# First attention of a fused attention and feed-forward kernel: q's transposes issued beside k's, and the third chunk's exponentials ahead of a norm's logarithm

## The chip, the cores and the metric

The kernel runs on one core of a Trainium2 chip. The metric is the device time of one execution in microseconds (us). Three executions before the change took 1340.37, 1340.40 and 1341.75 us; their median is 1340.4 us. The engines are named as in the profile: PE is TensorE (its weight loads are PEld), DVE is VectorE, ACT is ScalarE, POOL is GpSimd, and SP is SyncE, whose queue issues most of the DMAs.

## The reference, cut to what matters

```python
def rmsnorm(x, g):
    return x / np.sqrt(np.mean(x * x, axis=-1, keepdims=True) + 1e-06) * g
q_n, k_n = rmsnorm(q, g_q), rmsnorm(k, g_k)          # (8, 12, 448, 64)
scores = np.matmul(q_n, k_n.transpose(0, 1, 3, 2)) / np.sqrt(64)
attn = softmax(scores)                               # max, exp, sum + 1e-09, division
x = np.matmul(attn, v)                               # -> (3584, 768), heads side by side
...
h = np.maximum(x @ w_in, 0.0)                        # w_in (768, 2048)
out = (h * h) @ w_out                                # w_out (2048, 768)
```

Everything is float32. There are 8 batches of 12 heads; two heads of 64 columns fill the 128 partitions, so attention is done in 48 pairs of heads, six pairs to a batch.

## The kernel before, in words

The work is staged in four spans of two batches each. The **first attention** (`attention_alone`, L945) handles the 12 pairs of span 0 by itself on PE. Then each span's two products of the feed-forward follow, and the attention of the next span is threaded through the second product of the span before it. The products use one level of a Strassen-like scheme, whose weight blocks are prepared on DVE, ACT and POOL by the generator `prepare` (L556), a "tick" at a time; the first 48 ticks are spread over the first attention, the others over the first product.

The order of the instructions on each engine is the order in which the program issues them: nothing is rescheduled. Each engine works through its own queue in that order, and engines wait for one another by semaphores. So the place of a call in `attention_alone` sets its place in every engine's queue.

Within the first attention, the loop at L948 makes one **run** for each pair `i`; "the third run" is `i = 2`. A pair has 448 queries and keys, and the keys are cut into four chunks of 112. One run, from `i = 1` on, has four steps with a `yield` after each; after each `yield` the caller (L1502) issues the weight ticks that have come due.

- Step A: the loads of pair `i + 3` (on SP); `scores(i, 0)` and `scores(i, 1)`, each of which puts the scores of a chunk into a score bank by PE and then takes the exponentials of its two heads by ACT (L816 and L820); k's four transposes of the next pair, `transpose(i + 1, 1, 0)` (PE L791, then ACT's copy into `qkT`, L793); `values(i - 1, (2, 3))`, the second half of the previous pair's product of probabilities and v (PE L879); `add_up(i, 1)` (DVE L833, the sum of probabilities for the softmax's denominator); and `norm(i + 2)`, whose square is on ACT (L731) and whose sum and scaling are on DVE (L732, L733).
- Step B: q's four transposes of the next pair, `transpose(i + 1, 0, 0)` (PE L791), and ACT's copy with the gain (L795); `load_v(i + 1)` (SP L713); and `roots(i + 2)`: the logarithm and the exponential that make a reciprocal square root (ACT L742, L743), three small DVE instructions that refine it (L744 to L746), and the product that normalises q (POOL L747).
- Step C: `scores(i, 2)` and `scores(i, 3)`; `total_of(i - 1)` (PE L904, the denominators of the previous pair); `values(i, (0, 1))`; and `finish(i - 1)` on DVE (L922 to L924 make the factors, and L928 multiplies the value bank by them into `xT`).
- Step D: `add_up(i, 2)` for odd `i` (DVE L833), and `combine_x(i - 1)` (DVE, only from pair 6 on).

PSUM holds eight banks of 128 x 512 float32. The scores take two double banks in turn (`ps_s`, tag `s`): chunks 0 and 2 use one and chunks 1 and 3 the other. `ps_o` has one bank with the tag `o` and one with the tag `t` (for the totals). `ps_m` has the banks `m` and `n`; `bank(name, 0)` gives `m` and `bank(name, 1)` gives `n`. The values of an even pair are summed in `o`, those of an odd pair in `n` (L872). Both transposes, k's and q's, use bank `m`, one after the other. A bank is taken over by a new tile only when the last reader of the old one is done.

Of the kernel before, what the change touches and what calls it, by code (L numbers as in the profile page):

```python
# [10 lines left out]
F32 = mybir.dt.float32  # L11
U32 = mybir.dt.uint32
AF = mybir.ActivationFunctionType
# [331 lines left out]
def chunk_of(pt, s, j, n):  # L345

    return pt.rearrange("d (j p) -> d j p", j=n)[:, j] if s else pt.rearrange("d (p j) -> d j p", j=n)[:, j]
# [45 lines left out]
def attention_then_ffn_bounded(  # L393
# [35 lines left out]
    nc = tc.nc  # L429

    B, H, S, D = q.shape
    NT, DM = out.shape
    DFF = w_in.shape[1]
    P = 128
# [26 lines left out]
    ps_o = ctx.enter_context(tc.tile_pool(name="ps_o", bufs=1, space=bass.MemoryType.PSUM))  # L461
# [3 lines left out]
    def bank(name, n=None):  # L465

        turn[0] += n is None
        return ps_m.tile([P, S], F32, tag="mn"[turn[0] % 2 if n is None else n], name=name)

    qk, qkT, ident, mhalf, gains, rstd0, _ = held  # L470
# [209 lines left out]

    pts = {}
    vs, probs, pavs, tots, normed, rstds = {}, {}, {}, {}, {}, {0: rstd0}
    places, halves, rests = [], [], {}
    sums = {"out": [dram.tile([2 * S // 32, 32], F32, name=f"factors{n}") for n in range(2)]}

    def load(i):
        if i < NAT:
            load_q(nc, qk, q, i)
            load_k(nc, qk, k, i)
            return  # L690

        load_part(i, 0)
        load_part(i, 1)
# [15 lines left out]
    def load_v(i):  # L709
        b, h0 = i // NPAIR, 2 * (i % NPAIR)  # L710
        vs[i] = loads.tile([P, 2, NJ, D], F32, tag="vt", name="vt")
        if i < NAT:
            nc.sync.dma_start(vs[i][:SP].rearrange("p h j d -> p h (j d)"),  # L713
                              v[b, h0:h0 + 2].rearrange("h (p j) d -> p h (j d)", j=NJ))
        else:
            for h in range(2):
                nc.sync.dma_start(vs[i][:, h, 0:NF], v[b, h0 + h, 0:NF * P].rearrange("(j p) d -> p j d", j=NF))
            for rows in sides:
                nc.sync.dma_start(vs[i][rows, :, NF], v[b, h0:h0 + 2, NF * P:].rearrange("h p d -> p h d"))
# [66 lines left out]

    def transpose(i, s, n):

        pt = bank("pt", n)
        for j in range(NJ):  # L790
            nc.tensor.transpose(chunk_of(pt, s, j, NJ), normed[i][s][:, j * P:(j + 1) * P], ident[:SP, :SP])  # L791
        if s:
            nc.scalar.copy(qkT[:, i % 2, s], pt)  # L793
        else:
            nc.scalar.activation(qkT[:, i % 2, s], pt, AF.Copy, scale=gains[:, 0:1])  # L795

    def scores(i, c):


        if i >= NAT:  # L800
            sc = ps_s.tile([P, 2, 512], F32, tag="s", name="sc")
            n = S if c < NF else S // 2
            for h in range(2):
                rows = slice(h * D, (h + 1) * D)
                for m, part in enumerate(sides):
                    keys = slice(c * P + m * D, c * P + (m + 1) * D) if c < NF else slice(NF * P, S)
                    of = slice(0, S) if c < NF else slice(m * n, (m + 1) * n)
                    nc.tensor.matmul(sc[part, h, 0:n], qkT[rows, 0, 1, keys], qkT[rows, 0, 0, of], start=True, stop=True)  # L808
            pr = probs[i, c] = places[(NF * i + c) % len(places)] if c < NF else halves[i % 2]
            nc.scalar.activation(pr, sc[:, :, 0:n], AF.Exp)  # L810
            return
        at = i % 2
        sc = ps_s.tile([SP, 2, 512], F32, tag="s", name="sc")
        for h in range(2):
            rows = slice(h * D, (h + 1) * D)
            nc.tensor.matmul(sc[:, h, 0:S], qkT[rows, at, 1, c * SP:(c + 1) * SP], qkT[rows, at, 0, :],  # L816
                             start=True, stop=True)
        pr = probs[i, c] = places[(NJ * i + c) % len(places)][:SP]
        for h in range(2):
            nc.scalar.activation(pr[:, h], sc[:, h, 0:S], AF.Exp, scale=rstds[i][:, 1, 2 * c + h:2 * c + h + 1])  # L820
# [4 lines left out]
    def add_up(i, c):  # L825

        acc = acc_of(i)
        if i >= NAT and c == NF:
            for m, rows in enumerate(sides):
                part = acc[rows, :, m * S // 2:(m + 1) * S // 2]  # L830
                nc.vector.tensor_tensor(part, part, probs[i, c][rows], ALU.add)
            return
        nc.vector.tensor_tensor(acc, probs[i, 0] if c == 1 else acc, probs[i, c], ALU.add)  # L833
# [38 lines left out]
    def values(i, chunks=range(NJ)):  # L872
        if 0 in chunks:
            pavs[i] = ps_o.tile([P, S], F32, tag="o", name="pav") if i >= NAT or i % 2 == 0 else bank("pav", 1)
        if i >= NAT:
            return later_values(i)
        for c in chunks:
            for h in range(2):
                nc.tensor.matmul(pavs[i][h * D:(h + 1) * D, :], vs[i][:SP, h, c, :], probs[i, c][:, h, :],  # L879
                                 start=(c == 0), stop=(c == NJ - 1))  # L880

    def later_values(i):

        rests[i] = ps_o.tile([P, S], F32, tag="t", name="rest")
        for c in range(NF + 1):
            for h in range(2):
                for m, rows in enumerate(sides):
                    into = (rests[i] if m else pavs[i])[h * D:(h + 1) * D]
                    into = into if c < NF else into[:, m * S // 2:(m + 1) * S // 2]
                    nc.tensor.matmul(into, vs[i][rows, h, c, :], probs[i, c][rows, h, :],  # L890
                                     start=(c == 0), stop=(c == NF), skip_group_check=True)

    def added(i):

        return 3 if i % 2 and i + 1 < NAT else 2
# [16 lines left out]
    def finish(i):  # L912

        b, hp = divmod(i, NPAIR)
        x = factors = xT[:, b % 2, hp]
        if i < NAT:
            pav = pavs.pop(i)


            turned, factors = sums["turned"], sums["factors"]  # L920
            few = small.tile([P, S // 32], F32, tag="few", name="few", bufs=1)
            nc.vector.transpose(turned, tots.pop(i))  # L922
            nc.vector.reciprocal(few, turned.rearrange("p (g r) -> p g r", r=32)[:, :, 0])
            nc.vector.transpose(factors.rearrange("p (g r) -> p g r", r=32),  # L924
                                few.rearrange("p g -> p g ()").to_broadcast([P, S // 32, 32]))
        else:
            pav = rests.pop(i)
        nc.vector.tensor_tensor(x, pav, factors, ALU.mult)  # L928
        del vs[i]
# [15 lines left out]
    def attention_alone():  # L945


        for i in range(NAT):  # L948
            more = i + 1 < NAT
            if 0 < i < NAT - 3:  # L950
                load(i + 3)
            scores(i, 0)
            scores(i, 1)
            if i == 0:

                transpose(1, 1, 1)
                scores(0, 2)
                scores(0, 3)
                transpose(1, 0, 0)
                add_up(0, 1)  # L960
                norm(2)
                load_v(1)
                values(0, (0, 1))
                load(3)
                yield
                continue
            if more:
                transpose(i + 1, 1, 0)
            values(i - 1, (2, 3))
            add_up(i, 1)  # L970
            if i + 2 < NAT:
                norm(i + 2)
            elif not more:
                norm(NAT)
            yield
            if more:
                transpose(i + 1, 0, 0)
            if more:
                load_v(i + 1)
            if i + 2 < NAT:  # L980
                roots(i + 2)
            yield
            scores(i, 2)
            scores(i, 3)
            total_of(i - 1)
            values(i, (0, 1))
            finish(i - 1)
            yield
            if added(i) == 3:
                add_up(i, 2)  # L990
            combine_x(i - 1)
            if NAT <= i + 3 < NAT + 2:
                load(i + 3)
            yield
        values(i, (2, 3))
        total_of(i)
        finish(i)
        combine_x(i)

    def attention(first):  # L1000
# [3 lines left out]
        for i in range(first, last + 1):  # L1004
# [42 lines left out]
            if i > first:  # L1047
                finish(i - 1)
                combine_x(i - 1)
# [512 lines left out]
def kernel(  # L1562
# [49 lines left out]
    with tc.If(bits <= limit) as small_scores:  # L1612
        with tc.manual_schedule():
            attention_then_ffn_bounded(tc, *args, held)
# [32 lines left out]
```

## Time and profile before

| quantity | value |
|---|---|
| median of three executions | 1340.4 us |
| the profiled execution, its own time | 1337.88 us |
| its span, first to last instruction | 1336.1 us |
| PE busy | 1321.4 us (99%) |
| DVE, POOL, ACT busy | 855.1, 680.1, 486.2 us |
| PE in the first attention, first score to the first product's first matmul | 8.95 to 128.47 us |
| runs `i = 2` to `i = 10`, from the first score of one to that of `i = 11` | 25.89 to 115.73 us |

The span is shorter than the execution's own time by 1.8 us, which lie outside the first and the last instruction. PE's first score matmul of a run marks where the run begins. A matmul in float32 is two PE instructions, so the eight rows "x8" of a timeline line are four matmuls, that is two chunks of scores. The profile's end times for PE are modelled, so a stall of PE is read from the starts of its instructions.

### The profile page before, as it was taken

What the parts mean: (1) busy time and instruction counts of PE and PEld (TensorE: products, weight loads), DVE (VectorE), ACT (ScalarE), POOL (GpSimd) and SP (SyncE); (2) the same over time, 40 slices, a digit from 0 to 9 for tenths busy, and PEclk for the clock granted to TensorE, in tenths of its full rate; (3) what the DMA queues carried; (4) which work ended last, traced back from release to release, by engine and by line L of the source; (5) the groups of instructions that cost most, each with busy time, mean ns of one, the idle gap of its engine ahead of it and who ended that gap; (6) DMA issues with size and microseconds to landing.
All of it is one profiled execution on the core that took longest, in us unless ns stands there. A gap on an engine that the chain in (4) does not pass through costs nothing.

```text
span 1336.1 us, 17758 instructions
## 1 busy us (share of the span) xinstructions
PE 1321.4 (99%) x5930; PEld 698.9 (52%) x5930; DVE 855.1 (64%) x1334; ACT 486.2 (36%) x939; POOL 680.1 (51%) x544
## 2 busy tenths in 40 slices
PE   8999999999999999999999999999999999999997
PEld 3333455444446654444444755444444665556887
DVE  6998899489988233467887523457878723336553
ACT  7885656554540012255542011235554101111000
POOL 5677534467656222557774422448675522322452
PEclk9999999999999999999999999999999999999999
DMA  8887999656664433356655433345664444331333
GB/s 222 228 216 190 347 387 330 197 120 136 139 147 119 89 87 88 99 120 134 135 133 144 96 97 88 99 108 114 140 130 129 116 88 145 126 89 48 116 103 57
DMA packets 413817, 190.18 MB, mean 142 GB/s; under 512 B 282388, under 2 KB 408724, under 8 KB 413716
## 3 DMA queue, kind: packets, MB, share of 16 engines
q1 hardware_dynamic: 406164, 180.21, 51.6%
q0 software_dynamic: 4736, 8.40, 2.4%
q8 instruction: 49, 0.80, 0.3%
q10 hardware_dynamic: 2816, 0.34, 0.2%
q14 instruction: 52, 0.43, 0.1%
HBM read 155.72 MB, written 33.16 MB: 141 GB/s over the span
## 4 chain that ended last, share of the span: by engine, by line
PE 90%; DVE 4%; ACT 3%; DMA 1%; issue 1%; POOL 1%; SPq 0%; ACTq 0%; POOLq 0%
PE ps L1204 19%; PE pd L1104 11%; PE pa L1104 10%; PE pc L1104 10%; PE sc L808 7%; PE pav L890 6%; PE pb L1104 5%; PE ps L1387 3%; PE ps L1255 3%; PE pd L1359 2%; PE pc L1359 2%; PE pa L1359 2%; PE sc L816 1%; PE pd L1189 1%; PE pc L1189 1%; PE pa L1189 1%
## 5 line engine op out<-in xcount | busy, mean ns | idle before, releaser
L1076 POOL TENSOR_TENSOR gT<-gT 128x448 f32<-128x448 f32 x96 | 93.7, 978 | 258.5 <-ACT gT L1072 258.5
L773 POOL TENSOR_TENSOR half<-half,mhalf 128x28 f32<-128x28 f32 x36 | 184.8, 5133 | 69.9 <-DVE half L772 60.3
L1204 PE MATMUL ps<-gT,sw 128*128 128x448 f32 x432 | 169.3, 545 | 0.0
L1072 ACT ACTIVATE gT<-gT 128x448 f32<-128x448 f32 x96 | 55.3, 576 | 293.7 <-DVE gT L1120 293.6
L1104 PE MATMUL pa<-xT,sw 128*128 128x448 f32 x384 | 154.9, 539 | 0.0
L1204 PEld LDWEIGHTS ps<-gT,sw 128*128 128x128 f32 x432 | 80.1, 190 | 87.2 <-issue 84.6
L1204 PE MATMUL ps<-gC,sw 128*128 128x448 f32 x288 | 113.1, 546 | 0.0
L808 PE MATMUL sc<-qkT 64*64 64x448 f32 (+1 forms) x1152 | 110.2, 497 | 0.5 <-ACT pr L810 0.2
L1104 PEld LDWEIGHTS pa<-xT,sw 128*128 128x128 f32 x384 | 72.9, 190 | 70.6 <-issue 70.6
L588 POOL TENSOR_TENSOR gC<-gC 128x384 f32<-128x384 f32 x64 | 71.5, 1134 | 59.9 <-DVE gC L584 58.2
L1204 PEld LDWEIGHTS ps<-gC,sw 128*128 128x128 f32 x288 | 53.2, 190 | 59.5 <-issue 58.4
L858 POOL DMA_DIRECT2D xT<-factors x72 | 37.9, 531 | 89.1 <-DMA factors<-square 62.1
L1120 DVE TENSOR_TENSOR gT<-z,pd 128x448 f32<-128x448 f32 x32 | 19.9, 620 | 98.9 <-PE pd L1104 98.7
L810 ACT ACTIVATE pr<-sc 128x896 f32<-128x896 f32 x87 | 76.9, 909 | 11.8 <-PE sc L808 11.8
L775 POOL TENSOR_TENSOR qk<-qk,half 128x448 f32<-128x448 f32 x72 | 77.4, 1096 | 2.8
L1104 PE MATMUL pd<-xT,sw 128*128 128x448 f32 x192 | 77.8, 541 | 0.2
L1104 PE MATMUL pd<-xC,sw 128*128 128x448 f32 x192 | 77.5, 540 | 0.0
L1104 PE MATMUL pc<-xT,sw 128*128 128x448 f32 x192 | 77.4, 539 | 0.0
L1104 PE MATMUL pc<-xC,sw 128*128 128x448 f32 x192 | 77.4, 539 | 0.0
L1104 PE MATMUL pb<-xC,sw 128*128 128x448 f32 x192 | 77.4, 539 | 0.0
L890 PE MATMUL pav<-pr,vt 64*64 64x448 f32 x348 | 72.7, 537 | 0.0
L890 PE MATMUL rest<-pr,vt 64*64 64x448 f32 x348 | 72.7, 537 | 0.0
(282 smaller groups left out, 2447.6 us busy)
## 6 DMA issues: line engine op xcount, KB each, us to landing
sw<-w1s SPq DMA_DIRECT2D x224, 192.0 KB, 2.4
sw<-w2s SPq DMA_DIRECT2D x102, 256.0 KB, 3.4
w1s<-gC SPq DMA_DIRECT2D x8, 1344.0 KB, 7.0
w2s<-gC SPq DMA_DIRECT2D x8, 1344.0 KB, 6.1
qk<-in_q_dram SPq DMA_DIRECT2D x144, 56.0 KB, 2.5
qk<-in_k_dram SPq DMA_DIRECT2D x144, 56.0 KB, 2.3
xT<-factors POOLq DMA_DIRECT2D x72, 112.0 KB, 3.4
words<-in_moe_w_out_dram SPq DMA_DIRECT2D x9, 768.0 KB, 7.1
```

The costliest lines, as they stand in the source:

```text
L588: nc.gpsimd.tensor_tensor(*[blocks_of(n)[:, place_of(n, i)] for i in (dst, x, y)], op)
L773: nc.gpsimd.tensor_tensor(half, half, mhalf, ALU.pow)
L775: nc.gpsimd.tensor_tensor(qkn[:, s], raw[:, s], half[:, s * NG:(s + 1) * NG].rearrange("p g -> p g ()").to_broadcast([P, NG, 32]), ALU.mult)
L808: nc.tensor.matmul(sc[part, h, 0:n], qkT[rows, 0, 1, keys], qkT[rows, 0, 0, of], start=True, stop=True)
L810: nc.scalar.activation(pr, sc[:, :, 0:n], AF.Exp)
L890: nc.tensor.matmul(into, vs[i][rows, h, c, :], probs[i, c][rows, h, :], start=(c == 0), stop=(c == NF), skip_group_check=True)
L1072: nc.scalar.activation(g, src, AF.Relu)
L1076: nc.gpsimd.tensor_tensor(g, g, g, ALU.mult)
L1104: nc.tensor.matmul(ps, stream[n + at][:, c], rhs[:, c], start=first and c == 0, stop=c == HC - 1, skip_group_check=not first)
L1189: nc.tensor.matmul(ps, lhs[:, c], rhs(c), start=start and c == 0, stop=c == HK - 1, skip_group_check=not start)
L1204: nc.tensor.matmul(ps, stream[n][:, c % 4], rhs_of[i][:, c], start=c == 0, stop=c == HF - 1)
L1359: nc.tensor.matmul(ps, lhs[:, c], rhs[:, c], start=first and c == 0, stop=c == HK - 1, skip_group_check=not first)
```

## The change

It does two things, both in the first attention.

First, from the third run on (`i > 1`), q's transposes of pair `i + 1` are issued right after k's, ahead of `values(i - 1, (2, 3))`. They go into another bank than k's: for an even pair into `n`, for an odd pair into `o`, which is the bank in which that run's values are summed afterwards. ACT's copy with the gain stays where it was, at the head of step B, as the new function `gain`.

Second, in every run from `i = 1` on, `scores(i, 2)` is issued in step B, between `load_v(i + 1)` and `roots(i + 2)`, in place of at the head of step C.

The renaming of `turned` to `flat` in `finish` has no effect; it frees the name.

```diff
-    places, halves, rests = [], [], {}
+    places, halves, rests, turned = [], [], {}, {}
...
     def transpose(i, s, n):
 
-        pt = bank("pt", n)
+        if n is None:
+            pt = bank("pt", 1) if i % 2 == 0 else ps_o.tile([P, S], F32, tag="o", name="pt")
+        else:
+            pt = bank("pt", n)
         for j in range(NJ):
             nc.tensor.transpose(chunk_of(pt, s, j, NJ), normed[i][s][:, j * P:(j + 1) * P], ident[:SP, :SP])
         if s:
             nc.scalar.copy(qkT[:, i % 2, s], pt)
+        elif n is None:
+            turned[i] = pt
         else:
-            nc.scalar.activation(qkT[:, i % 2, s], pt, AF.Copy, scale=gains[:, 0:1])
+            gain(i, pt)
+
+    def gain(i, pt):
+        nc.scalar.activation(qkT[:, i % 2, 0], pt, AF.Copy, scale=gains[:, 0:1])
...
             if more:
                 transpose(i + 1, 1, 0)
+                if i > 1:
+                    transpose(i + 1, 0, None)
             values(i - 1, (2, 3))
...
             if more:
-                transpose(i + 1, 0, 0)
+                if i > 1:
+                    gain(i + 1, turned.pop(i + 1))
+                else:
+                    transpose(i + 1, 0, 0)
             if more:
                 load_v(i + 1)
+            scores(i, 2)
             if i + 2 < NAT:
                 roots(i + 2)
             yield
-            scores(i, 2)
             scores(i, 3)
             total_of(i - 1)
```

More of the change, by code (lines that the diff above doesn't have):

```diff
@@ L917, in finish @@
             pav = pavs.pop(i)
-            turned, factors = sums["turned"], sums["factors"]
+            flat, factors = sums["turned"], sums["factors"]
             few = small.tile([P, S // 32], F32, tag="few", name="few", bufs=1)
-            nc.vector.transpose(turned, tots.pop(i))
-            nc.vector.reciprocal(few, turned.rearrange("p (g r) -> p g r", r=32)[:, :, 0])
+            nc.vector.transpose(flat, tots.pop(i))
+            nc.vector.reciprocal(few, flat.rearrange("p (g r) -> p g r", r=32)[:, :, 0])
             nc.vector.transpose(factors.rearrange("p (g r) -> p g r", r=32),
```

## The prediction

> **What bounds the kernel now.** I read the page first, for the bounding engine.
>
> ```profile
> PE 1321.4 (99%) x5930; PEld 698.9 (52%) x5930; DVE 855.1 (64%) x1334; ACT 486.2 (36%) x939; POOL 680.1 (51%) x544
> PEclk9999999999999999999999999999999999999999
> ```
>
> PE is busy for 99% of the span at full clock. So time is won only where PE stands still or does superfluous work. Next come the waits of PE, over the whole span.
>
> ```profile
> PE pt L791 <- ACT qkT L793: 2.3, 5, 1.3
> PE sc L816 <- ACT gT L820: 0.6, 1, 0.6
> ```
>
> The first line is PE at q's transposes: they share k's bank, so they wait for ACT's copy of k. The second is PE at a run's second chunk of scores, waiting for old exponentials. Because PE's ends are modelled, I then looked at its starts in run 2 (`i = 2`; runs are named by `i`), the worst one, and at ACT there.
>
> ```profile
> 27.58 0.60 PE L791 MATMUL pt<-ident,qk 112*128 112x112 f32 x4
> 28.11 1.72 PE L879 MATMUL pav<-gT,vt 112*64 112x448 f32 x8
> 31.15 0.57 PE L791 MATMUL pt<-ident,qk 112*128 112x112 f32 x4 [1.31 <-ACT qkT L793]
> 31.65 1.76 PE L816 MATMUL sc<-qkT 64*112 64x448 f32 x8
> ```
> ```profile
> 30.46 0.54 ACT L793 COPY qkT<-pt 128x448 f32<-128x448 f32 x1
> 30.87 1.09 ACT L731 ACTIVATE qk<-qk 112x1024 f32<-112x1024 f32 x1
> 31.83 0.65 ACT L795 ACTIVATE qkT<-pt,gains 128x448 f32<-128x448 f32 x1
> 33.46 0.21 ACT L742 ACTIVATE half<-rstd 112x16 f32<-112x16 f32 x1 [0.98 <-DVE rstd L733]
> ```
>
> The values start at 28.11 and normally hold PE for 1.65 (as 38.73 to 40.38 in run 3). Here q's transposes begin 3.04 later, because ACT reaches k's copy at 30.46: a stall of 1.39. On ACT, the logarithm waits 0.98 for DVE while exponentials stand behind it. Last, busy times of runs 2, 3, 8 and 9 show who else is near the limit.
>
> ```profile
> 25.90:36.50 10.60, 9.29 (x50) 3.58 (x49) 9.80 (x17) 9.18 (x17) 3.85 (x5) 1.00 1.13 311
> 36.50:46.50 10.00, 10.00 (x54) 3.88 (x52) 8.15 (x14) 8.64 (x17) 6.11 (x6) 1.00 1.00 246
> 85.65:95.60 9.95, 9.34 (x52) 3.61 (x50) 9.71 (x16) 6.96 (x14) 7.90 (x6) 1.00 0.85 227
> 95.60:106.10 10.50, 10.26 (x52) 3.79 (x52) 10.29 (x15) 8.40 (x16) 8.72 (x9) 1.00 0.69 222
> ```
>
> Columns: stretch, length, then busy PE, PEld, DVE, ACT, POOL. DVE has 0.2 us to spare in runs 8 and 9, 0.8 in run 2. Over runs 2 to 10 it is busy 82.1 of 89.8, so it is the next bound.
>
> **What the Trainium skill says.** "Perfetto Trace Analysis", Tensor Engine Instruction: PE's end is estimated, not observed. The trace agrees: run 5's second chunk of scores comes 0.2 late, though PE appears busy there. "PSUM — Partial Sum Buffer", Engine vs sequencer instructions: ACT, DVE and POOL queues are strict FIFO, and matmuls start in program order. The trace agrees: ACT's idle 0.98 at 33.46 lies in front of work that was ready. The same page, PSUM bank collisions: two engines must be kept apart per bank, not per address. So q's transposes must wait until DVE has read the old values out of their new bank; no row of before shows that wait. "SBUF — State Buffer", Who interferes with whom: a DVE instruction with two SBUF inputs contends with POOL's reads. The trace agrees: L833 takes 1.09 at its best and 1.89 at 99.65, beside POOL's work.
>
> **The change, part by part.** An undisturbed run, from score to score, takes 9.26 with eight total instructions (run 6: 66.37 to 75.63) and 10.02 with twelve (run 7: 75.63 to 85.65). Runs 2 to 10 have five of the first and four of the second: 5 x 9.26 + 4 x 10.02 = 86.38. They took 115.73 - 25.89 = 89.84, so 3.46 is stall: 1.35 in run 2, 0.04 in run 4, 0.54 in 5, 0.67 in 8, 0.54 in 9, 0.33 in 10.
>
> *q's transposes beside k's.* No instruction is added or removed: 4 transposes and one gain copy move, 9 times over. What goes is (a) the wait for k's copy, and (b) a change of kind on PE. A group of four starts at 48.20, .36, .45, .55 and gives way at 48.74: steps of 0.152, 0.095, 0.096 and 0.189, so 0.535 alone. Eight together should take 0.152 + 6 x 0.096 + 0.189 = 0.92 instead of 1.07, a saving of 0.15 a run, 1.35 in all. The trace has no eight together, so the bounds are 0 (change of bank as dear as change of kind) and 1.35; no reason makes it a loss. I take 1.35. What comes is a wait for the new bank's previous user, L928 of `finish(i - 2)`. Behind it on PE stand the values and everything later. The normed q is no limit: POOL's L747 ends at 55.92 in run 4 and is wanted at 58.3 in run 5. The gain copy keeps its place on ACT, and the values that reuse the bank come over 3 us behind it. SP's queue issues the same loads in the same order; v's load waits for values that end 0.9 later in the run, but is wanted a run later.
>
> *Third chunk's exponentials ahead of the logarithm.* Two exponentials (half of the 2.18 of four, so 1.1) fill ACT's wait for DVE: 9 waits, 10.3 us. The last chunk's exponentials then end about 1.1 earlier, and the next run's copies with them. The price: where the sums are ready early, the logarithm waits for those exponentials, and L744 holds DVE. From ACT's order this is 0.6 in run 5, 0.8 in 6 and 1.2 in 7, where a weight tick precedes the gain; elsewhere DVE's sums come later anyway.
>
> *What is late next.* I placed the rows of runs 2 to 10 anew with their old durations, PE by 9.11 or 9.86 a run. Run 2 loses its whole stall, and run 3 starts at 35.00 instead of 36.50. There q's transposes meet L928, which DVE, busy without a break, still ends at 37.37: 0.27 of waiting. Run 4 starts at 45.15 (was 46.51) and run 5 at 54.26 (55.81). Again L928: in the old trace it ran from 58.28 to 58.90; DVE, a full queue, is 2.05 earlier, so 56.85 against PE's 56.4: 0.45. Run 6 starts at 64.65 (66.37), run 7 at 73.76 (75.63), waiting 0.35 for L928 at 76.2. Run 8 starts at 84.0 (85.65), run 9 at 93.11 (95.58), where the second chunk waits 0.45 for exponentials that hang on DVE's sums. Run 10 starts at 103.4 (106.14) and waits 0.3 for L928. Run 11 starts at 112.85 (115.73). In it, DVE comes 0.3 late with the last norm's sums, and the last exponentials are just in time today (125.26 against 125.32): 0.3 more. So 3.46 + 1.35 = 4.81 are to be had, and 0.27 + 0.45 + 0.35 + 0.45 + 0.3 + 0.3 = 2.12 come back as new waits: 2.7. Rounding of the placing lets it be 2.6 to 2.9; I take **2.8**.
>
> *After it.* From 128 us PE has hardly a gap, and DVE waits for PE in the first product (8.5 + 5.4 + 3.7 + 3.2 us), so the lead is kept. The profiled execution would go from 1337.9 to 1335.1. The median lies 2.5 above it, without a row that says why; the same 2.8 off gives 1340.4 - 2.8 = **1337.6**.
>
> **The rivals.** *Full gain:* DVE's L833 runs nearer to 1.09 because POOL's rows now fall elsewhere, L928 is never late, and all 4.8 is kept: 1335.6. For it: DVE idles 7.7 us over the nine runs. Against: it idles hardly at all from 45 to 64 us. *Bank instead of copy:* DVE doesn't move earlier, and the wait for L928 takes the place of that for k's copy. Run 2's 1.4 stays won (L928 ends there at 27.43, before 28.1), with little else: 1339.0. For it: DVE's full runs 2, 5, 8 and 9. *Slower:* the logarithm behind the exponentials holds DVE at L744 in each of runs 2 to 9, the eight of these that have a norm. DVE has (89.8 - 82.1) / 8 = 0.96 for each to spare; a hold above that makes DVE the bound. At 1.2 each, as worked out for run 7, DVE would need 82.1 + 8 x 1.2 = 91.7, so 1.9 more than now: 1342.3. Against: in five of the eight DVE's sums are ready no earlier than the exponentials end. *No effect:* the order of the queues is the program's, so the change does what it says.
>
> **How the numbers follow.** Forecast 1337.6 (1336.6 to 1338.4): 0.5. Full gain: 0.19. Bank instead of copy (1338.4 to 1340.2): 0.24. Slower: 0.07. The range from 1335.4 to 1340.3 leaves out the slower case and a little at the edges. About 0.2%, 2.7 us, is what a measurement can tell from no change: 1337.7. Somewhat over half of the forecast's chance and all of the full gain lie below it: 0.50 faster; 0.44 within; 0.06 slower.
>
> **What would show it.** Right: no PE wait at L791 for L793 from run 2 on; runs of 9.1 and 9.9; exponentials ahead of L742 on ACT; new PE waits at L791 for DVE L928 in runs 3, 5, 7, 10. The first score of run 11 comes near 112.9 and the first product near 125.8. Wrong: eight transposes taking 1.07; waits for L928 above 0.5 a run; DVE idle before L744 by more than 0.9; or a lead at 128 us that is gone by 260.

## The result, and the profile after

| quantity | before | after |
|---|---|---|
| median of 19 executions each | 1339.64 us | 1338.00 us |
| ratio, 95% interval | | 0.9987 (0.9981 to 0.9993) |
| span of the profiled execution | 1336.1 us | 1334.6 us |
| first score to first product (the first attention) | 119.52 us | 117.49 us |
| start of run 2 to start of run 11 | 89.84 us | 87.82 us |
| last matmul's start to the end of the span | 8.29 us | 9.22 us |

The change gains 1.6 us in the medians, and its interval allows 0.9 to 2.5 us. The forecast was 2.8 us. So the direction was right and the size too large: the first attention itself became 2.03 us shorter, and the rest of the difference to 1.6 lies within the interval. The level of 1337.6 us was met within 0.4 us partly by luck: the three executions of before that it started from had their median 0.8 us above that of all 19. The gain is under the 0.2% that the prediction took as the least a measurement can tell from no change; with 19 executions each, the interval leaves out zero all the same.

First the page's line of busy times, and the busy times of runs 2 to 10 (length, then PE, PEld, DVE, ACT, POOL), both of after.

```profile
PE 1319.8 (99%) x5930; PEld 699.0 (52%) x5930; DVE 856.0 (64%) x1334; ACT 486.4 (36%) x939; POOL 678.7 (51%) x544
```
```profile
25.77:113.59 87.82, 85.78 (x450) 33.29 (x448) 82.34 (x124) 75.72 (x135) 61.99 (x47) 1.00 0.85 238
```

The counts are the same as before: nothing was added. DVE has as much to do as before (82.34 against 82.10) in 2 us less, so it has come nearer to being the bound. The waits of PE from 8 to 130 us in the profile after (columns: waiting engine, tile and line, who it waited for, total us, times, longest). L794 is now the transposes, L824 the scores, L828 the exponentials, L936 the last instruction of `finish`.

```profile
PE pt L794 <- DVE xT L936: 1.2, 1, 1.2
PE sc L824 <- ACT gT L828: 0.8, 2, 0.6
PE sc L824 <- ACT qkT L389: 0.8, 1, 0.8
PE pt L794 <- ACT qkT L796: 0.3, 1, 0.3
```

The wait for L389 belongs to run 0 and is 0.8 in both kernels. The 2.3 us for k's copy have shrunk to one wait of 0.3, in run 1 (at 19.63), which keeps the old order. In their place stands one wait of 1.2 us for DVE. PE's timeline in run 2 shows the gain.

```profile
25.77 1.76 PE L824 MATMUL sc<-qkT 64*112 64x448 f32 x8
27.46 0.99 PE L794 MATMUL pt<-ident,qk 112*128 112x112 f32 x8
28.38 1.72 PE L887 MATMUL pav<-gT,vt 112*64 112x448 f32 x8
30.03 1.76 PE L824 MATMUL sc<-qkT 64*112 64x448 f32 x8
31.72 1.72 PE L912 MATMUL tot<-gT,ones 112*64 112x448 f32 x8
```

The eight transposes take 28.38 - 27.46 = 0.92, and nothing in the run waits. ACT beside it:

```profile
31.34 1.18 ACT L828 ACTIVATE gT<-sc,rstd 112x448 f32<-112x448 f32 x2
32.80 0.21 ACT L742 ACTIVATE half<-rstd 112x16 f32<-112x16 f32 x1 [0.28 <-DVE rstd L733]
```

Two exponentials now fill what was an idle 0.98, of which 0.28 is left. PE's timeline in run 5 shows the loss.

```profile
53.85 1.76 PE L824 MATMUL sc<-qkT 64*112 64x448 f32 x8
55.54 0.60 PE L794 MATMUL pt<-ident,qk 112*128 112x112 f32 x4
57.35 0.57 PE L794 MATMUL pt<-ident,qk 112*128 112x112 f32 x4 [1.21 <-DVE xT L936]
57.85 1.72 PE L887 MATMUL pav<-gT,vt 112*64 112x448 f32 x8
```

The group of eight is torn apart. Four of the eight take 0.44 up to the start of the next one, so q's half could have begun at 55.98; it began at 57.35 and stood still for some 1.4 us. DVE's timeline at that place says why.

```profile
52.76 0.55 DVE L613 TENSOR_SCALAR gC<-gC 128x768 uint32<-128x768 uint32 x1
53.35 1.68 DVE L618 SCALAR_TENSOR_TENSOR gC<-words,gC 128x768 uint32<-128x768 uint32 x1
54.95 0.64 DVE L930 STREAM_TRANSPOSE gT<-tot 128x448 f32<-128x448 f32 x1
55.62 0.24 DVE L931 RECIPROCAL few<-gT 128x14 f32<-128x14 f32 x1
55.90 0.65 DVE L932 STREAM_TRANSPOSE gT<-few 128x448 f32<-128x448 f32 x1
56.58 0.62 DVE L936 TENSOR_TENSOR xT<-pav,gT 128x448 f32<-128x448 f32 x1
```

DVE has no gap here, and two instructions that prepare weights (L613 and L618, of the two ticks that are due here) stand ahead of the `finish` that frees the bank. L936 ends at 57.20 and PE goes on 0.15 later.

Where the 2.02 us come from, by runs (length from score to score in us; in the fourth row, what the new order takes without a stall):

| run | 2 | 3 | 4 | 5 | 6 | 7 | 8 | 9 | 10 | sum |
|---|---|---|---|---|---|---|---|---|---|---|
| before | 10.61 | 10.01 | 9.30 | 10.56 | 9.26 | 10.02 | 9.94 | 10.55 | 9.59 | 89.84 |
| after | 9.11 | 9.86 | 9.11 | 11.26 | 9.11 | 9.94 | 9.11 | 10.75 | 9.58 | 87.82 |
| undisturbed | 9.11 | 9.86 | 9.11 | 9.86 | 9.11 | 9.86 | 9.11 | 9.86 | 9.11 | 84.99 |

Stall was 3.46 before and is 87.82 - 84.99 = 2.83 after. So the transposes' saving (1.39 with the lengths of this table) is two thirds of the gain, and only 0.63 of the stall has gone, though its places have changed wholly: runs 2 and 8 are free of it, runs 5 and 9 have more than before. The lead is kept: from the first product's start to the last matmul, before takes 1199.32 and after 1199.06. The last row of the first table then takes 0.93 back in this one profile; it is 8.36 in another profile of the same kernel (e8), and lies between 7.12 and 9.22 us over all profiles told here.

### The profile page after: what moved, and what is told of

Its sections match the earlier page's. It is cut to its first block, busy times and chain, and to the rows that moved or that the text cites. A ratio compares the mean times of both kernels' runs of the same rounds, so it can differ in the third digit from the quotient of the medians.

```text
span 1334.6 us, 17767 instructions
## 1 busy us (share of the span) xinstructions
PE 1319.8 (99%) x5930; PEld 699.0 (52%) x5930; DVE 856.0 (64%) x1334; ACT 486.4 (36%) x939; POOL 678.7 (51%) x544
## 4 chain that ended last, share of the span: by engine, by line
PE 93%; DVE 3%; ACT 2%; issue 1%; DMA 1%; POOL 0%; SPq 0%; ACTq 0%
PE ps L1217 21%; PE pd L1117 11%; PE pa L1117 10%; PE pc L1117 10%; PE sc L816 7%; PE pav L898 7%; PE pb L1117 5%; PE ps L1400 3%; PE ps L1268 3%; PE pd L1372 2%; PE pc L1372 2%; PE pa L1372 2%; PE sc L824 2%; PE pav L887 2%; PE pd L1202 1%; PE pa L1202 1%
## 5 line engine op out<-in xcount | busy, mean ns | idle before, releaser
L1217 PEld LDWEIGHTS ps<-gT,sw 128*128 128x128 f32 x432 | 80.1, 190 | 87.1 <-issue 85.3
L1117 PE MATMUL pd<-xC,sw 128*128 128x448 f32 x192 | 77.5, 540 | 0.0
L1117 PE MATMUL pc<-xC,sw 128*128 128x448 f32 x192 | 77.5, 540 | 0.0
```

The source lines that it names most:

```text
L1117: nc.tensor.matmul(ps, stream[n + at][:, c], rhs[:, c], start=first and c == 0, stop=c == HC - 1, skip_group_check=not first)
L1217: nc.tensor.matmul(ps, stream[n][:, c % 4], rhs_of[i][:, c], start=c == 0, stop=c == HF - 1)
```

## The experiments

The theory after the result: PE's stall is not removed but handed to the next queue; in run 5 it is DVE's order that sets it. The rival: that wait is small or chance, and the gain is limited by something else (DVE's total work, late exponentials, or a load).

**The two parts apart.** e1 is the changed kernel with `scores(i, 2)` put back behind the roots:

```diff
-            scores(i, 2)
             if i + 2 < NAT:
                 roots(i + 2)
             yield
+            scores(i, 2)
             scores(i, 3)
```

> The first part alone: q's transposes stand beside k's in another bank, and the third chunk's exponentials stay behind the logarithm. The measure is PE's time from its first score to the first product's first matmul: 119.52 us before, 117.49 us with both parts (2.03 less). Theory (three engines are near their limit, and each part removes some of the same stalls): run 2 loses its 1.35 of stall, eight transposes together save 0.15 in each of nine runs, and the late exponentials in runs 8 to 10 remain; with a wait for L928 in run 5 that makes 117.9, 1.6 less than before, and about 1338.4 us where before is 1340. Rival (the place is the whole gain): 117.5 or less. Rival (the exponentials are the whole gain): 119.4.

e2 is the kernel before with only the exponentials moved:

```diff
+            scores(i, 2)
             if i + 2 < NAT:
                 roots(i + 2)
             yield
-            scores(i, 2)
             scores(i, 3)
```

> The second part alone: the third chunk's scores and exponentials ahead of the logarithm, q's transposes behind the values in k's bank as before. Theory: ACT reaches k's copies about 1 us earlier, so the wait for them shrinks from 1.35 to 0.35 in run 2 and goes in runs 5, 9 and 10; nothing waits for L928; exponentials that hang on DVE's sums cost 1.2 in runs 9 and 10. First score to first product 117.5 to 118.0, so 1.5 to 2.0 less than before, nearly what both parts together give: the parts replace each other more than they add. Rival (the place is the whole gain): 119.4. Rival (the gains add up, 2.0 together): 119.1 if the first part alone gives 1.6.

| kernel | runs 2 to 10 | median, before beside it | ratio, 95% interval |
|---|---|---|---|
| e1, transposes only | 89.21 (0.63 gained) | 1339.58, 1339.51 | 1.0000 (0.9992 to 1.0008) |
| e2, exponentials only | 88.83 (1.01 gained) | 1338.10, 1339.51 | 0.9989 (0.9983 to 0.9995) |

PE's waits from 8 to 130 us, of e1 and then of e2:

```profile
PE sc L824 <- ACT gT L828: 1.5, 2, 0.9
...
PE pt L794 <- DVE xT L936: 0.6, 1, 0.6
PE pt L794 <- ACT qkT L796: 0.3, 1, 0.3
PE pav L887 <- DMA vt<-in_v_dram: 0.3, 1, 0.3
```
```profile
PE pt L791 <- ACT qkT L793: 1.9, 4, 1.2
PE sc L816 <- ACT qkT L389: 0.8, 1, 0.8
PE sc L816 <- ACT gT L820: 0.4, 1, 0.4
```

Moving the transposes does take the copy's wait away from run 2 on, but the exponentials are then late (1.5 us, in runs 4 and 8), run 2 loses 0.47 by the starts to the load of v, and so little is left that the median shows none of it. Moving the exponentials alone takes 0.4 us off the copy's waits, and nearly all of the wait in run 2 stays (1.16). There ACT comes earlier to an instruction that waits for a load of weights, and its wait grows from 0.41 before to 1.26:

```profile
27.51 0.92 ACT L594 ACTIVATE gC<-gT 128x768 f32<-128x768 f32 x1 [1.26 <-DMA gT<-in_moe_w_in_dram]
```

So k's copy begins at 30.39 instead of 30.46. It is the bank of its own that frees PE from this copy: e1 and e3 have no such wait in run 2. The parts gain 0.63 and 1.01 alone, 1.64 in sum, and 2.02 together. That they help one another is not shown, since the second pair of profiles (e8 and e11 below) gives 1.67 for the two together.

**The bank without the place.** e3 keeps the separate bank, but issues q's transposes where they stood on PE before, behind the values:

```diff
                 transpose(i + 1, 1, 0)
-                if i > 1:
-                    transpose(i + 1, 0, None)
             values(i - 1, (2, 3))
+            if more and i > 1:
+                transpose(i + 1, 0, None)
             add_up(i, 1)
```

> Both parts, but q's transposes, still in the bank of the values, stand behind the values of the previous pair as before the change: the bank is new, the place is old. The wait for k's copy is gone by the bank alone. Theory: the wait for DVE's product in run 5 (1.21) goes, because PE comes 1.65 later to the bank; the change of kind costs 0.15 in each of nine runs again; together 117.4 to 117.7, about what both parts give (117.49). Rival (the place beside k's is what counts): 118.8 or more. Rival (DVE sets the pace in run 5 whatever PE waits for, so that the wait only turns up later): 118.6.

Measured: runs 2 to 10 take 88.18, the median is 1337.06 beside 1339.51, the ratio 0.9982 (0.9975 to 0.9988). Run 5 takes 10.01, so no wait for L936 is left there: the values ahead of q's transposes cover it. The saving of 0.15 a run is gone (runs of 9.26 and 10.01), and run 2 takes 10.09. PE's timeline there shows a wait that the prediction had not priced:

```profile
30.99 0.60 PE L794 MATMUL pt<-ident,qk 112*128 112x112 f32 x4
31.52 1.76 PE L824 MATMUL sc<-qkT 64*112 64x448 f32 x8
33.21 1.72 PE L912 MATMUL tot<-gT,ones 112*64 112x448 f32 x8
35.55 1.72 PE L887 MATMUL pav<-gT,vt 112*64 112x448 f32 x8 [0.61 <-DMA vt<-in_v_dram]
```

This v was issued in run 1, whose transposes the change leaves alone. It took 10.7 us to land, and PE lost 0.79 by the starts; in the kernel after the same load took 9.0, landed at 32.38 and was wanted at 33.27. Run 2 of e6, whose order is that of the change up to run 7, lost 0.23 at the same place, with a load of 9.9; both profiles are among those with a long run 0 (last section). So this wait varies without the edit, and how much of it is e3's own is not shown. From run 3 to run 10 e3 takes 78.09, and the change 78.71 and 79.00 (after and e8). In time e3 does no worse than the change itself (the intervals of the ratios overlap), so the place beside k's isn't shown to be worth anything over the bank alone: what it saves on PE it pays largely to DVE in run 5.

**The wait in run 5.** If it is DVE's order, `finish` ahead of the weight tick in that one run takes it away (e5; the yield that lets the tick in comes behind `finish` when `i` is 4):

```diff
                 roots(i + 2)
-            yield
+            if i != 4:
+                yield
             scores(i, 3)
             total_of(i - 1)
             values(i, (0, 1))
             finish(i - 1)
+            if i == 4:
+                yield
             yield
```

> Both parts, and in run 4 alone the closing of the previous pair on DVE (L930 to L936) is issued ahead of the weight tick that stood in front of it; the work is the same. Theory (in run 5 PE waits for L936 because of DVE's order, two weight instructions of 2.2 us in front of it, and not because of the amount of DVE's work): run 5 falls from 11.26 to 9.9, no wait for L936, first score to first product about 116.1 against 117.49 with both parts. Rival (DVE is full, and what is pushed back there is paid later): run 5 shorter, but runs 6 to 9 longer by as much; 117.2 to 117.6.

DVE's timeline in e5, and PE's:

```profile
54.71 0.62 DVE L936 TENSOR_TENSOR xT<-pav,gT 128x448 f32<-128x448 f32 x1
55.25 0.58 DVE L613 TENSOR_SCALAR gC<-gC 128x768 uint32<-128x768 uint32 x1
55.87 1.67 DVE L618 SCALAR_TENSOR_TENSOR gC<-words,gC 128x768 uint32<-128x768 uint32 x1
```
```profile
54.00 1.76 PE L824 MATMUL sc<-qkT 64*112 64x448 f32 x8
55.69 0.98 PE L794 MATMUL pt<-ident,qk 112*128 112x112 f32 x8
56.61 1.72 PE L887 MATMUL pav<-gT,vt 112*64 112x448 f32 x8
```

L936 ends at 55.33, before PE asks, and the eight are together again: run 5 takes 9.86 instead of 11.26. ACT's and POOL's instructions of the two ticks move as well, but DVE had no gap in front of L936 in after, and the two rows that stood there now stand behind it. Of the 1.40, 0.4 comes back in run 6 (9.52 instead of 9.11) and 0.3 in run 7 (10.24 instead of 9.94), where PE now waits 0.2 each for L936 and a group is torn apart again. Runs 2 to 10 take 86.85. The one time taken was 1334.70. e12 is the same kernel, timed:

> Both parts with the closing of pair 3 ahead of the weight tick in run 4 alone, timed: the first look gave 116.51 from first score to first product, 0.98 less than both parts. Theory: the time follows, 0.9979 to 0.9983 of before, where both parts alone gave 0.9987 and 0.9989. Rival (the first look was luck of the early loads): 0.9987 or more.

Measured: 1336.56 beside 1339.24, ratio 0.9979 (0.9971 to 0.9987); runs 2 to 10 take 86.86, so 2.98 us less than before. This shows the cause of the largest new wait. e12 has the lowest ratio of all that were timed, though its interval overlaps those of e3 and e7, and of the change itself.

**The next wait, in runs 9 and 10.** In run 9 of after, PE's second chunk of scores waits for exponentials (0.62 at 94.90). Putting the last chunk's exponentials ahead of the logarithm too, for late runs only, should help if ACT's order is the cause (e6); the rival was that DVE then comes late instead. e7 joins e5 and e6.

```diff
             scores(i, 2)
+            if i > 7:
+                scores(i, 3)
             if i + 2 < NAT:
                 roots(i + 2)
             yield
-            scores(i, 3)
+            if i <= 7:
+                scores(i, 3)
```

> Both parts, and from run 8 on the fourth chunk's scores and exponentials also stand ahead of the logarithm. There ACT waits 1.8 and 2.1 us for DVE's sums, with the fourth chunk's exponentials behind. Theory: the waits of PE in runs 9 and 10 (0.89 and 0.47 over 9.86 and 9.11) go, DVE isn't held because its sums come later than the exponentials end, and first score to first product is about 116.2. Rival (the waits in 9 and 10 come from DVE being late as such): they come back as waits for the product L936 or for the gain copies, and it stays 117.2 to 117.5.

> Both parts with both of the other orders: the closing ahead of the tick in run 4, and the fourth chunk ahead of the logarithm from run 8 on. Theory: the stalls of runs 2 to 10 fall from 2.83 to about 0.2, first score to first product about 114.9, and the time is 0.9967 of before, near 1335.0 us. Rival (a third engine or v's loads set the pace at once): 116 or more, and 0.998.

In e6 the wait for exponentials is gone, and q's transposes wait instead. PE's timeline in run 9, then DVE's:

```profile
96.42 0.60 PE L794 MATMUL pt<-ident,qk 112*128 112x112 f32 x4
97.58 0.57 PE L794 MATMUL pt<-ident,qk 112*128 112x112 f32 x4 [0.56 <-POOL gC L580]
```
```profile
96.81 0.62 DVE L936 TENSOR_TENSOR xT<-pav,gT 128x448 f32<-128x448 f32 x1
```

The profile names POOL as the releaser, but L936 ends at 97.43 and PE starts 0.15 behind it, as in run 5: it is DVE. Run 9 takes 10.61 instead of 10.75, so the rival was right. e6's runs 2 to 10 take 87.86 (one time, 1338.00); e7's take 86.77, with a median of 1336.47 beside 1338.70, ratio 0.9983 (0.9976 to 0.9989). The stall that is left in runs 2 to 10 is 1.78, where 0.2 was expected: the second order adds nothing that shows.

**Is it DVE's amount of work?** e4 leaves out the third chunk's part of the denominators of odd pairs, which removes five L841 instructions from these runs:

```diff
             yield
-            if added(i) == 3:
-                add_up(i, 2)
             combine_x(i - 1)
```

> Both parts, but DVE doesn't add the third chunk's probabilities to the sum for the odd pairs 1 to 9: their denominators lack that chunk, and DVE has five instructions of 1.1 to 1.9 us less to do in the first attention. PE and ACT do the same work. Theory (DVE is the next bound, and both the wait for its product in run 5 and the late exponentials of runs 8 and 9, which hang on its sums, come from its queue): the stalls of runs 2 to 10 fall from 2.83 to 0.3 or less, and first score to first product is 115.0 to 115.4. Rival (ACT is the next bound): 117 to 117.5, with waits of PE for exponentials as long as now.

Measured: runs 2 to 10 take 87.08, only 0.74 less than after (one time, 1335.40). This was a miss. The five instructions at the line's mean of 1.67 are 8.4 us of DVE, but DVE's busy time fell only from 82.34 to 77.58: its other instructions became longer by some 3.6. For example, the first L946 (in `combine_x`) went from 0.61 to 1.09 and the L608 behind it from 0.55 to 1.37, while two L580 on POOL beside them went from 4.16 to 2.69. Over runs 2 to 10 POOL's busy time fell from 61.99 to 56.67 with the same 47 instructions. So, as these rows read, part of the time that DVE gave up went to POOL, and DVE's next rows paid for it. e9 takes POOL's work away instead and leaves DVE's instructions as they are: the weight words 4 to 11 are not computed on POOL, and their blocks keep old contents.

```diff
             _, eu, low, _ = parts(n)
+            if 4 <= n < 12:
+                return
             if n < EARLY // 4:
...
-            if there(n) and n % 2:
+            if there(n) and n % 2 and not 4 < n < 12:
```

> Both parts, with POOL's work on the weight words 4 to 11 left out (L580 and L588), so that POOL has hardly anything but L747 in runs 6 to 10, and the weight blocks that it would have made are stale. Theory (in runs 7 to 10 DVE is late because its instructions with two inputs wait for POOL, 1.9 us in place of 1.1 for L841): L841 takes 1.1 to 1.3 in runs 6 to 10, DVE gains 3 to 5 us in them, PE's waits for the fourth chunk's exponentials in runs 9 and 10 go (10.75 and 9.58 become 9.9 and 9.15), and first score to first product is about 116.2 against 117.5 to 117.8. Rival (DVE's lateness is its own order of work, not POOL): runs 9 and 10 stay above 10.5 and 9.4.

The line of the sums of probabilities from 62 to 115 us (duration in ns as min/median/max), in after and in e9, where it is L843:

```profile
L841 DVE TENSOR_TENSOR gT<-gT x8: 1315/1775/1903, 65.9 to 109.5; 112x896 f32<-112x896 f32 x8
```
```profile
L843 DVE TENSOR_TENSOR gT<-gT x8: 1080/1091/1528, 66.2 to 106.7; 112x896 f32<-112x896 f32 x8
```

And the busy times from 25.8 to 113 us, in after and in e9 (length, then PE, PEld, DVE, ACT and POOL):

```profile
25.80:113.00 87.20, 85.16 (x448) 33.26 (x448) 81.76 (x123) 75.10 (x135) 61.45 (x46) 1.00 0.85 237
```
```profile
25.80:113.00 87.20, 85.81 (x452) 33.75 (x452) 75.78 (x126) 76.05 (x136) 30.21 (x25) 1.00 0.84 239
```

With POOL's work halved, DVE does three more instructions in 6.0 us less. Runs 9 and 10 take 9.86 and 9.11, exactly the undisturbed lengths, and from 24 to 126 us it is now DVE that waits for PE (4.8 us in all for the totals, against 0.4 in after). So in runs 9 and 10 the wait is the time that DVE loses beside POOL. Run 5 still takes 11.44, but e9 is no test of POOL there: the first words left out come later, and up to 58 us POOL is as busy as in after (20.10 and 20.04). For run 5 the evidence is e5. Whether POOL also lengthened DVE's rows on the way to run 5 (L618 took 1.68 at 53.35 and 0.95 at 92.31) was not tested. The Trainium skill's page "SBUF — State Buffer", Who interferes with whom, says that the pair of ports which DVE shares with GpSimd is an exclusive lock and the only place of such contention. The two rows of the sums agree that DVE is slower beside POOL; a whole lock they don't show.

**When is it slower?** e10 puts the last chunk's exponentials ahead of the logarithm in every run, so that the logarithm comes last: the mechanism of the prediction's slower rival, made stronger.

```diff
             scores(i, 2)
+            scores(i, 3)
             if i + 2 < NAT:
                 roots(i + 2)
             yield
-            scores(i, 3)
```

> Both parts, and in every run the fourth chunk's scores and exponentials too stand ahead of the logarithm. It tests the price of the hold on DVE: behind four exponentials in place of two, the logarithm comes about 1.1 later wherever DVE's sums are ready before, and L744 holds DVE in front of the closing of the pair. Theory (what delays DVE delays PE at L936): the waits of DVE for L743 grow from 0.2, 0.9 and 0.7 in runs 5 to 7 to 1.3, 2.0 and 1.8, and appear in runs 2 to 4 with 0.5 to 1.2; PE waits longer for L936; first score to first product 119 to 120.5 against 117.5 to 117.8. Rival (earlier exponentials make up for it): 117 to 118.

DVE's waits from 24 to 126 us (one line of after, then of e10), and PE's from 8 to 130 us in e10:

```profile
DVE other L744 <- ACT half L743: 2.4, 6, 0.9
```
```profile
DVE other L744 <- ACT half L743: 5.9, 7, 1.3
```
```profile
PE pt L794 <- DVE xT L936: 3.9, 3, 2.1
```

DVE is held 3.5 us more, `finish` comes later, and PE waits up to 2.1 for it. Runs 2 to 10 take 91.38, 1.54 more than before, and the one time is 1342.26 beside a median of 1339.24. So that rival's mechanism is real, but in the change the hold stays at 2.4 us in all and never passes 0.9.

**Both kernels again.** e8 is the changed kernel and e11 the kernel before, unchanged, to see what is chance.

> The changed kernel once more, beside the others. It shows how much of a run's length is chance: the early loads of the weights and of v land at other times in each execution, and ACT in run 2 waits for one of them. Theory: runs 3 to 10 repeat within 0.3 us in sum, runs 0 to 2 differ by up to 1.5 us. The time is 0.9980 to 0.9993 of before. Rival (all runs vary alike): runs 3 to 10 differ by over 1 us in sum.

> The kernel before once more, for its run 2: the stall of 1.35 there began with ACT waiting for a load of weights. Theory: that load lands at another time in each execution, so run 2 is anywhere from 9.3 to 10.7 here, while runs 3 to 10 repeat 79.23 within 0.3. Rival: run 2 is 10.5 to 10.7 again.

e8: runs 2 to 10 take 88.11, run 5 again 11.45; the median is 1336.88 beside 1338.70, ratio 0.9989 (0.9981 to 0.9997). e11: 89.78, with run 2 again 10.53; one time, 1340.85. So the stalls belong to the programs. In these two profiles the change gains 1.67 in runs 2 to 10, and the two measured gains of the median are 1.6 and 1.8.

## Why the prediction was right, and where not

- *PE is the bound and only its stalls and superfluous work can be won.* Right: the stall of before (3.46) came out as 3.40 in e11, and in every timed kernel the median moved by what runs 2 to 10 gained to within 0.9 us.
- *Eight transposes take 0.92.* Right to the hundredth, and with it the undisturbed runs of 9.11 and 9.86. It is the surest term of the sum.
- *The wait for k's copy goes.* Right from run 2 on.
- *Two exponentials fill ACT's wait.* Right in sign. Late in run 9 they don't reach far enough: the logarithm still waited 2.08 for DVE's sums (at 102.77), the last chunk's exponentials stood behind it, and PE waited 0.21 for exponentials in run 10 (at 105.23).
- *v's load "is wanted a run later".* Right, but how long such a load takes was not priced. The one that is issued in run 1 and wanted in run 2 takes 9.0 in the change, lands 0.9 ahead of need and costs nothing; in e1 and e3 it takes 10.1 and 10.7 and costs 0.47 and 0.79 by the starts.
- *The new waits give 2.12 back* is **the term that was wrong**, by its size: in runs 2 to 10 it had 1.82, and 2.83 (in e8 about 3.1) was measured. Its kinds were right, a wait for DVE's last row of `finish` and late exponentials, though run 10's was put down to the first and came from the second. One of the prediction's own signs of being wrong, a wait for L928 above 0.5 in a run, came in run 5. The waits of runs 3, 7 and 11 are smaller or absent (0, 0.08 and 0 against 0.27, 0.35 and 0.3), but run 5 has 1.40 against 0.45, run 9 0.89 against 0.45, run 10 0.47 against 0.3.

Run 5 can be taken apart. The prediction had L928 end at 56.85 and PE ask at 56.4. PE asked at 55.98, 0.4 earlier, since run 3 had not waited. L936 ended at 57.20, 0.35 later: run 4's `finish` was taken to come 2.05 earlier than before and came 1.70 earlier, because in run 3 DVE still waited 0.38 for PE's totals (it was paced by PE, not "a full queue"), and from one `finish` to the next DVE has 11.58 us of work (45.62 to 57.20). DVE's row in run 3:

```profile
43.35 0.65 DVE L930 STREAM_TRANSPOSE gT<-tot 128x448 f32<-128x448 f32 x1 [0.38 <-PE tot L912]
```

The 0.15 from DVE's end to PE's start was not counted at all. Together 0.45 + 0.4 + 0.35 + 0.15 = 1.35 of the 1.40.

For run 9 the old durations were a poor guide. Two sums of probabilities on DVE ahead of it took 1.65 and 1.67 us (at 77.5 and 85.3), where before they took 1.09 and 1.16 (at 78.9 and 86.4). That fits the 0.44 by which run 9's wait was too small, and e9 removes this wait; that these two rows alone made the difference isn't shown.

So time won in runs 2 to 4 was partly lost in run 5, and e5 shows that the order on DVE's queue decided it. Of the rivals, "full gain" fails, since L841 became no shorter (mean 1.67 after, 1.64 before): e9 shows what it would have needed. "Bank instead of copy" has the right mechanism for run 5, but not for the whole; e1, with less gain than it forecast, loses more to late exponentials (1.5) than to L936 (0.6). "Slower" is e10.

Open: whether e3, the bank without the place, is better than the change. In its one profile it gained 0.36 us less in runs 2 to 10, but run 2's wait for v cost it 0.79 there, and from run 3 on it was 0.6 to 0.9 faster; its median is at least as good. The intervals overlap.

## What to carry to other kernels

When a stall on the bounding engine is removed, follow that engine's new arrival time to the next instruction that it shares a buffer with, and read the in-order queue that frees this buffer: an unrelated instruction ahead of the release there can take a part of the gain, and moving it was worth another 1.0 us in runs 2 to 10 here, on top of the change's 2.0. Before calling two edits more or less than their sum, profile the same kernel twice: here the change gave 2.02 and 1.67. And don't place one engine's rows by their old durations when they may slide beside POOL's: here DVE's row went from 1.09 to 1.78 us by that alone.

## What was not expected of the hardware

Three of the profiles (e3, e6, e11) begin with a run 0 of 7.7 us instead of 6.5, whatever the edit. The busy times from 9 to 12 us, of before and of e11, show why in the last columns (after POOL: granted clock, DMA share, GB/s):

```profile
9.00:12.00 3.00, 2.95 (x16) 1.31 (x16) 0.86 (x2) 2.91 (x6) 2.43 (x2) 1.00 0.76 189
```
```profile
9.00:12.00 3.00, 3.00 (x8) 0.99 (x8) 0.86 (x2) 2.05 (x4) 2.43 (x2) 0.50 0.83 190
```

TensorE's granted clock was 0.50 there, and PE's first eight rows of scores took 3.33 us instead of 1.76. The Trainium skill's page "TensorE: Matmul & The Clock Gate", Part 1, says that the array runs at half its clock when idle and until it has been busy for about 3.4 us, and that a free-running window makes the number of slow matmuls vary from run to run. These rows agree with the half clock and with the chance; the 3.4 us they don't test. A long run 0 puts 1.2 us of chance into an execution, over half of what the change gains, and is a reason to compare runs 2 to 10 and not the whole first attention.
